# One transfer order, shared score banks and split masks in a fused attention and two-MLP kernel

## The chip, the cores and the metric

The kernel runs on one core of a Trainium2 chip. The metric is the device time of one execution in microseconds; the figure for a kernel is the median of its runs. Below, TensorE, VectorE, ScalarE and GpSimd are the compute engines (PE, DVE, ACT and POOL in the profile), and SP is the engine whose queue issues all transfers between main memory (HBM) and the on-chip memory. TensorE writes its results to eight banks of accumulator memory (PSUM), from which VectorE and ScalarE read them.

## What is computed

```python
# q, k, v: 4 batches, 8 heads, 768 positions, 64 values; weights of the MLPs come as 64-bit floats
k_sum = k.reshape(B, H, nb, 32, D).max(axis=3)        # one key per block of 32
v_sum = v.reshape(B, H, nb, 32, D).mean(axis=3)       # one value per block of 32
scores_l = where(|i - j| < 16, q @ k.T / sqrt(D), -1e9)
scores_s = q @ k_sum.T / sqrt(D) + log(32)
a = softmax(concatenate([scores_l, scores_s]))
x = a @ concatenate([v, v_sum])                       # to 3072 tokens x 512
h = max(max(x @ w1, x @ w2), x @ w3)                  # 768 wide
x2 = h @ w_out
h2 = x2 @ w_in2                                       # 2048 wide
out = (h2 * tanh(softplus(h2))) @ w_out2              # 3072 x 512, fp32
```

A position sees only its neighbours within 15 positions and the 24 block summaries of its batch.

## The kernel before

**Attention.** The 3072 tokens form 24 steps `u` of 128 tokens, six to a batch; a step is two tiles of 64 queries. A tile's keys are a window of 96 positions and 24 block keys, `KX` = 120 columns. `s2(u)` (L427) makes the scores of 8 heads: 32 small fp32 products into the score tile `sc`, then the row maxima `nm` (VectorE) and eight exponentials with their sums (ScalarE). The mask is added in one of two ways. For `u < PEMASK` = 3, TensorE first puts it into `sc` by a product of the identity and the mask (L435), and the scores accumulate on it. From step 3 on, VectorE adds it while it moves the scores to `s` (L452). `s2b` divides by the sums (VectorE for six steps, then GpSimd), `s3` transposes the weights (`ptp`, copied to `pT`), `s4` multiplies by values (`xp`) and splits the result into a rounded part `xh` and a rest `xl`, both fp32r, TensorE's rounded format.

**Numbers in two parts.** Every weight and activation of the MLPs is such a pair, and a product of two is made of three matmuls (high by high, high by low, low by high). `run_job` (L195) brings a weight tile through stages: `fetch` (transfer into `words`, three buffers), `size_of` (ScalarE), `narrow` (VectorE), and a last stage. The first 14 jobs (`PEJOBS`) rebuild the low part by three TensorE products in a bank `wp` (L232 to L234). The second MLP's weights are split in the same way and stored to `w2d` (L256, L257).

**Keys, queries, values.** `load_nat` brings 128 positions into one of four `nat` buffers; `q_prep` and `k_prep` transpose them (`tp`). For batches after the first, `k_prep` copies the transposed keys to `kst`, a single buffer, and stores them to `kTd` (L360); `load_k` later brings a tile's window from there (L396). `v_prep` makes block means of the second batch's values by TensorE (`vp`), copies them to `vc`, which uses the same buffer as `kst`, and stores them to `vsd` (L310). For batches 2 and 3, `make_vsum` makes the means on GpSimd and VectorE. `load_v` brings value windows into four buffers `vr`.

**The MLPs.** The first runs in eight blocks of 384 tokens: `gemm1` with three products `hp` for each of six slices, and `gemm2` with four products `yp`, stored to `x2d` (L623). The second MLP follows: `g3` (product `up`), `mish_a` to `mish_c` (ScalarE and VectorE), `g4` (products `acc`, kept in three banks), and the store of `out`.

**Banks.** During attention: three in `gps` (tag "g": `wp`, `hp`, `yp`), three in `aps` (tag "a": `tp`, `vp`, `ptp`, `xp`) and one tile of two banks in `asc` for the scores. In the second MLP: `gps`, two in `ups`, and three for `acc`.

**Order.** Attention is written as a list of items, five to a step; `attend` emits them between the products of the MLP, about one block and four items ahead. `run_job` is called after every second item at first, before each product for the first two blocks, and before every third product after that. This is program order. A scheduler then places each engine's instructions by its own estimate of when they are ready, and each engine, SP's queue too, runs its own list strictly in that order. Transfers can so leave program order, but for two rules: `behind()` places query, key and value loads and the far key stores behind the last weight transfer while the weights of the first MLP come in, and an engine's instructions that need a buffer wait for its last readers.

Of the kernel before, what the change touches and what calls it, by code (L numbers as in the profile page):

```python
# [19 lines left out]
P = 128  # L20
# [33 lines left out]
def tile_kernel(ctx, tc, q, k, v, w1, w2, w3, w_out, w_in2, w_out2, out):  # L54
# [28 lines left out]
    gps = ctx.enter_context(tc.tile_pool(name="gps", bufs=3, space=PSUM))  # L83
# [43 lines left out]

    att = ExitStack()
# [27 lines left out]
    def fetch(src):  # L156
        words = stage.tile([P, 1024], U32, name="words", tag="words")
        o, x = src(words)
        last["words"] = nc.sync.dma_start(out=o, in_=x)
# [91 lines left out]
    def keep(f, i):  # L251
        def done(w, _):
# [3 lines left out]
            nc.sync.dma_start(out=w2d[f][:, 2 * i], in_=h.bitcast(F32))  # L256
            nc.sync.dma_start(out=w2d[f][:, 2 * i + 1], in_=w)  # L257
# [9 lines left out]
    def load_b(f, tl):  # L267
        wb[f] = tl
        nc.sync.dma_start(out=tl.bitcast(F32), in_=w2d[f])
# [21 lines left out]
    def load_nat(kind, src, b, g):  # L291
        t = ap3.tile([P, H, D], F32, name="nat", tag="nat", bufs=NATB)
        nat[kind, b, g] = t
        with behind() if "words" in last else nullcontext():
            nc.sync.dma_start(out=t, in_=src[b, :, g * P : (g + 1) * P, :].rearrange("h p d -> p h d"))
# [7 lines left out]
    def v_prep(b, g):  # L303
# [4 lines left out]
        vc = ap1.tile([P, H, D], F32, name="vc", tag="kst")[0:NS]  # L308
        nc.scalar.copy(vc, vp[0:NS])
        nc.sync.dma_start(out=vsd[b][:, g * NS : (g + 1) * NS, :].rearrange("h n d -> n h d"), in_=vc)  # L310
# [3 lines left out]
    def load_vsum(b, g, part):  # L314
# [3 lines left out]
        nc.sync.dma_start(out=t[0 : GRP * NB], in_=src[:, part])  # L318

    def make_vsum(b, g, part):  # L320
# [10 lines left out]
        if part == NPART - 1:  # L331
# [5 lines left out]
            nc.sync.dma_start(out=vsd[b][g * GRP : (g + 1) * GRP].rearrange("h n d -> (h n) d"), in_=vs[:, 0])  # L337
# [11 lines left out]
    def k_prep(b, g, st=None):  # L349
# [9 lines left out]
        if b:  # L359
            nc.sync.dma_start(out=kTd[b][:, :, g * P : (g + 1) * P], in_=st)  # L360

    def store_far():

        for g in range(NG):
            lo = max(g * P, NEAR * QT - HALO)
            if lo < (g + 1) * P:
                with behind():
                    nc.sync.dma_start(out=kTd[0][:, :, lo : (g + 1) * P], in_=kst[g][:, :, lo - g * P :])
# [17 lines left out]
    def load_k(T):  # L386
# [9 lines left out]
        nc.sync.dma_start(out=dst[:, :, o : o + hi - lo], in_=kTd[b][:, :, lo:hi])  # L396
# [3 lines left out]
    def load_v(T):  # L400
        b, t = divmod(T, TPS)
        dst = vr[T % RV]
        if T < NEAR:
            if T == 0:
                nc.sync.dma_start(out=dst[NB : NB + HALO], in_=vroom[0][0:HALO])
            for g, l, h, o in pieces(t):
                nc.sync.dma_start(out=dst[o : o + h - l], in_=vroom[g][l:h])
# [3 lines left out]
        nc.sync.dma_start(out=dst[o : o + hi - lo], in_=rows(lo, hi))  # L411

        if o > NB:
            nc.sync.dma_start(out=dst[NB:o], in_=rows(0, o - NB))
# [4 lines left out]
    def load_s(b):  # L419

        for t in vr:
            nc.sync.dma_start(out=t[0:NB], in_=vsd[b].rearrange("h n d -> n h d"))
# [4 lines left out]
    def s2(u):  # L427

        t = u % NG
        mask = masks["first" if t == 0 else "last" if t == NG - 1 else "mid"]  # L430
        sc = asc.tile([P, 2, 512], F32, name="sc", tag="sc")
        add = u >= PEMASK
        if not add:
            for r in range(2):
                nc.tensor.matmul(  # L435
                    sc[:, r, 0 : NP * KX], lhsT=ident, rhs=mask.unsqueeze(1).to_broadcast([P, NP, KX]),
                    start=True, stop=False,
                )
        for p in range(NP):
            for e in reversed(range(GT)):  # L440
                for r in range(2):
# [3 lines left out]
                        sc[c, r, p * KX : (p + 1) * KX], lhsT=qT[u % RQ][d, p, c], rhs=kT[(GT * u + e) % RK][d, p],  # L445
# [3 lines left out]
        src = sc[:, :, 0 : NP * KX].rearrange("q r (p x) -> q r p x", p=NP)  # L449
        if add:  # L450
            wide = mask.unsqueeze(1).unsqueeze(1).to_broadcast([P, 2, NP, KX])
            nc.vector.tensor_tensor(out=heads(s), in0=src, in1=wide, op=ALU.add)  # L452
# [432 lines left out]
```

## Time and profile before

| | |
|---|---|
| median of 3 runs | 1132.33 us (1130.82 to 1132.83) |
| profiled execution | 1133.17 us, span 1131.4 us, mean granted clock 0.994 |
| TensorE matmul | busy 1098.0 us, 97%, 7004 instructions |
| TensorE weight load | 987.8 us, 87% |
| VectorE | 812.4 us, 72%, 1595 instructions |
| ScalarE | 549.6 us, 49%, 1336 instructions |
| GpSimd | 75.8 us, 7%, 132 instructions |
| transfers | 125.49 MB, mean 111 GB/s |

The span reaches from the first instruction to the last; the execution's own time is a little longer. A busy share is a mean over stages that differ: the attention and the first MLP take the time to about 600 us, the second MLP the rest. In the rows shown below, PE is a matmul, PEld the load of its weights, SPq the issue of a transfer by SP; a time in brackets is how long the engine stood idle before the instruction, and behind the arrow is what ended that. A row of stages gives, for each engine, busy time in us and (in brackets) instructions, then the granted TensorE clock, the transfers' share of 16 DMA engines and GB/s. In rows of the chain, the numbers are start and duration. A row of waits has the total in us, the number and the longest.

### The profile page before, as it was taken

The numbers are of one execution on the slowest core, as the hardware profiler recorded it, in microseconds if no ns is written. First come the engines' busy times: TensorE is split into PE (matmuls) and PEld (weight loads), VectorE is DVE, ScalarE is ACT, GpSimd is POOL, SyncE is SP. The second block draws the span as 40 slices with busy tenths as digits, with TensorE's granted clock in tenths as the row PEclk, the third lists the DMA queues.
The fourth block names the chain that finished last, engine by engine and source line by source line (L and its number), as shares of the span: only waits on it lengthen the run. The fifth ranks groups of instructions, "written<-read, shape, count | busy, mean of one in ns | idle before, by whom it ended". The sixth has DMA issues, their size and how long they took to land.

```text
span 1131.4 us, 18637 instructions
## 1 busy us (share of the span) xinstructions
PE 1098.0 (97%) x7004; PEld 987.8 (87%) x7004; DVE 812.4 (72%) x1595; ACT 549.6 (49%) x1336; POOL 75.8 (7%) x132
## 2 busy tenths in 40 slices
PE   6888999999999899999999999999999999999998
PEld 3557889999898899999999998989889898999887
DVE  5678934287887789852238887787878888787775
ACT  4676535345544554632125554545545455454543
POOL 3000012211113110100000000000000000000000
PEclk9999999999999899999999999999999999999999
DMA  9897745466887857521557010100001010000000
GB/s 234 217 253 201 174 126 135 125 172 197 225 215 221 228 172 201 159 68 52 179 189 288 15 57 1 55 2 23 35 1 56 1 29 29 14 29 1 29 1 28
DMA packets 179730, 125.49 MB, mean 111 GB/s; under 512 B 125048, under 2 KB 161400, under 8 KB 177592
## 3 DMA queue, kind: packets, MB, share of 16 engines
q1 hardware_dynamic: 179640, 124.30, 39.0%
q8 instruction: 55, 0.90, 0.3%
q14 instruction: 35, 0.29, 0.1%
HBM read 88.05 MB, written 35.05 MB: 109 GB/s over the span
## 4 chain that ended last, share of the span: by engine, by line
PE 77%; DVE 10%; ACT 5%; DMA 4%; issue 3%; POOL 1%; SPq 0%; ACTq 0%; POOLq 0%; DVEq 0%
PE up L679 8%; PE up L677 8%; PE acc L732 8%; PE up L678 8%; PE acc L733 8%; PE acc L734 8%; PE hp L584 6%; PE hp L586 6%; PE hp L585 6%; ACT s L459 3%; PE yp L618 2%; PE yp L620 2%; PE yp L619 2%; PE xp L493 1%; DVE words L182 1%
## 5 line engine op out<-in xcount | busy, mean ns | idle before, releaser
L695 ACT ACTIVATE r<-n,two 128x384 f32<-128x384 f32 x128 | 78.9, 616 | 153.9 <-DVE n L692 153.9
L584 PE MATMUL hp<-xh,a 128*128 128x384 f32 x384 | 133.9, 349 | 6.3 <-ACT m L592 3.4
L586 PE MATMUL hp<-xh,a 128*128 128x384 f32 x384 | 129.3, 337 | 0.0
L585 PE MATMUL hp<-xl,a 128*128 128x384 f32 x384 | 129.3, 337 | 0.0
L718 DVE TENSOR_TENSOR gl<-g,gh 128x384 fp32r<-128x384 f32 x128 | 71.3, 557 | 64.2 <-ACT gh L717 63.8
L688 ACT ACTIVATE e<-up 128x384 f32<-128x384 f32 x128 | 63.0, 492 | 98.8 <-PE up L679 97.9
L584 PEld LDWEIGHTS hp<-xh,a 128*128 128x128 f32 x384 | 72.4, 188 | 11.1 <-ACT m L592 4.3
L459 ACT ACTIVATE s<-s,nm 128x120 f32<-128x120 f32 x168 | 64.0, 383 | 29.5 <-DVE nm L455 29.5
L705 DVE TENSOR_TENSOR p<-up,r 128x384 f32<-128x384 f32 x128 | 70.6, 552 | 5.5 <-ACT r L696 5.5
L585 PEld LDWEIGHTS hp<-xl,a 128*128 128x128 f32 x384 | 72.5, 189 | 0.8 <-issue 0.5
L586 PEld LDWEIGHTS hp<-xh,a 128*128 128x128 f32 x384 | 72.4, 189 | 0.1
L690 DVE TENSOR_SCALAR ep<-e 128x384 f32<-128x384 f32 x128 | 45.9, 358 | 35.8 <-ACT e L688 35.3
L710 DVE SCALAR_TENSOR_TENSOR g<-u,n 128x384 f32<-128x384 f32 x128 | 70.9, 554 | 0.8
L708 DVE SCALAR_TENSOR_TENSOR u<-u,p 128x384 f32<-128x384 f32 x128 | 70.7, 552 | 0.4
L692 DVE SCALAR_TENSOR_TENSOR n<-e,ep 128x384 f32<-128x384 f32 x128 | 70.7, 552 | 0.3
L707 DVE SCALAR_TENSOR_TENSOR u<-n,r 128x384 f32<-128x384 f32 x128 | 70.3, 549 | 0.0
L717 ACT CAST gh<-g 128x384 fp32r<-128x384 f32 x128 | 64.3, 502 | 9.4 <-DVE g L710 9.4
L584 PE MATMUL hp<-xh,b 128*128 128x384 f32 x192 | 67.8, 353 | 0.3 <-ACT y L622 0.3
L696 ACT ACTIVATE r<-r 128x384 f32<-128x384 f32 x128 | 67.1, 524 | 1.0
L618 PE MATMUL yp<-hh,c 128*128 128x384 f32 x192 | 65.6, 344 | 0.1
L677 PE MATMUL up<-x2h,a 128*128 128x384 f32 x192 | 64.5, 336 | 0.0
L678 PE MATMUL up<-x2l,a 128*128 128x384 f32 x192 | 64.5, 336 | 0.0
(167 smaller groups left out, 2886.0 us busy)
## 6 DMA issues: line engine op xcount, KB each, us to landing
words<-in_moe_w_out SPq DMA_DIRECT2D x22, 512.0 KB, 4.7
words<-in_moe_w SPq DMA_DIRECT2D x18, 512.0 KB, 5.3
words<-in_moe_w_in SPq DMA_DIRECT2D x16, 512.0 KB, 3.9
w2d<-wr SPq DMA_DIRECT2D x32, 256.0 KB, 4.6
w2d<-wa SPq DMA_DIRECT2D x32, 256.0 KB, 5.2
kT<-kTd SPq DMA_DIRECT2D x35, 192.0 KB, 5.1
vr<-in_v SPq DMA_DIRECT2D x35, 192.0 KB, 3.6
nat<-in_q SPq DMA_DIRECT2D x24, 256.0 KB, 4.3
```

Source lines behind the costliest of these rows:

```text
L459: nc.scalar.activation(out=s[:, h], in_=src[:, r, p], func=AF.Exp, bias=nm[:, r, p : p + 1], accum_out=sm[:, h : h + 1])
L584: nc.tensor.matmul(pt[:, :n], lhsT=wh, rhs=xh[:, c, :n], start=(c == 0), stop=False)
L585: nc.tensor.matmul(pt[:, :n], lhsT=wh, rhs=xl[:, c, :n], start=False, stop=False)
L586: nc.tensor.matmul(pt[:, :n], lhsT=wl, rhs=xh[:, c, :n], start=False, stop=(c == KC - 1))
L618: nc.tensor.matmul(pt[:, :n], lhsT=wh, rhs=hh[:, :n], start=(f == 0), stop=False)
L677: nc.tensor.matmul(pt[:, :N2], lhsT=wh, rhs=xh[:, c], start=(c == 0), stop=False)
L678: nc.tensor.matmul(pt[:, :N2], lhsT=wh, rhs=xl[:, c], start=False, stop=False)
L679: nc.tensor.matmul(pt[:, :N2], lhsT=wl, rhs=xh[:, c], start=False, stop=(c == KC - 1))
L695: nc.scalar.activation(out=r, in_=d["n"], func=AF.Ln, bias=two[:, 0:1])
L732: nc.tensor.matmul(o, lhsT=gh[:, c], rhs=w[:, 2], start=(f == 0), stop=False)
L733: nc.tensor.matmul(o, lhsT=gh[:, c], rhs=w[:, 3], start=False, stop=False)
L734: nc.tensor.matmul(o, lhsT=gl[:, c], rhs=w[:, 2], start=False, stop=(f == NF2 - 1))
```

## The change

- **Transfers.** Every transfer goes through a new function `dma`, which places it on SP behind the one before it in program order. `behind()` and `last["early"]` go. At the start, the products of the first scores and one weight job now stand ahead of the first two value loads.
- **Scores.** `sc` becomes two one-bank tiles from the pool `aps`, one for each half of the heads. `asc` goes, `aps` has four banks and `gps` four. VectorE's add, and for steps 0 to 2 its maximum, are done for each half.
- **Masks.** For steps 0 to 2 the mask is split once by VectorE into a rounded part and a rest, in buffers of later `hh5` and `hl5`, and TensorE adds both by fp32r products with the rounded identity `one_r`.
- **Value means.** `v_prep` writes `vc` into the first four partitions of the `nat` buffer that it has read.
- **Second MLP.** `ups` goes; all `up` tiles come from `gps`, four banks where there were five.

```diff
-    gps = ctx.enter_context(tc.tile_pool(name="gps", bufs=3, space=PSUM))
+    gps = ctx.enter_context(tc.tile_pool(name="gps", bufs=4, space=PSUM))
...
+    split_masks = {}
+    for kind, tag in (("first", "hh5"), ("mid", "hl5")):
+        both = gx.tile([P, MAXT * QT], F32R, name=f"both_{kind}", tag=tag)
+        h, l = both[:, 0:KX], both[:, KX : 2 * KX]
+        nc.vector.tensor_copy(h, masks[kind])
+        nc.vector.tensor_tensor(out=l, in0=masks[kind], in1=h.bitcast(F32), op=ALU.subtract)
+        split_masks[kind] = h, l
...
-    aps = att.enter_context(tc.tile_pool(name="aps", bufs=3, space=PSUM))
-    asc = att.enter_context(tc.tile_pool(name="asc", bufs=1, space=PSUM))
-    last = {"early": True}
+    aps = att.enter_context(tc.tile_pool(name="aps", bufs=4, space=PSUM))
+    last = {}
+
+    def dma(out, in_):
+        with tc.issue_after(last["dma"].ins) if "dma" in last else nullcontext():
+            last["dma"] = nc.sync.dma_start(out=out, in_=in_)
...
-        last["words"] = nc.sync.dma_start(out=o, in_=x)
+        dma(out=o, in_=x)
-    def behind():
-        return tc.issue_after(last["words"].ins) if last["early"] else nullcontext()
...
-        vc = ap1.tile([P, H, D], F32, name="vc", tag="kst")[0:NS]
+        vc = t[0:NS]
         nc.scalar.copy(vc, vp[0:NS])
...
-        sc = asc.tile([P, 2, 512], F32, name="sc", tag="sc")
+        sc = [bank("sc") for r in range(2)]
         add = u >= PEMASK
         if not add:
             for r in range(2):
-                nc.tensor.matmul(
-                    sc[:, r, 0 : NP * KX], lhsT=ident, rhs=mask.unsqueeze(1).to_broadcast([P, NP, KX]),
-                    start=True, stop=False,
-                )
+                for j, m in enumerate(split_masks[kind]):
+                    nc.tensor.matmul(
+                        sc[r][:, :, 0:KX], lhsT=one_r, rhs=m.unsqueeze(1).to_broadcast([P, NP, KX]),
+                        start=(j == 0), stop=False,
+                    )
...
         if add:
-            wide = mask.unsqueeze(1).unsqueeze(1).to_broadcast([P, 2, NP, KX])
-            nc.vector.tensor_tensor(out=heads(s), in0=src, in1=wide, op=ALU.add)
-            src = heads(s)
+            for r in range(2):
+                wide = mask.unsqueeze(1).to_broadcast([P, NP, KX])
+                nc.vector.tensor_tensor(out=heads(s)[:, r], in0=src[r], in1=wide, op=ALU.add)
+            src = [heads(s)[:, r] for r in range(2)]
...
-        nc.vector.tensor_reduce(out=nm, in_=src, axis=AX.X, op=ALU.max, negate=True)
+        if add:
+            nc.vector.tensor_reduce(out=nm, in_=heads(s), axis=AX.X, op=ALU.max, negate=True)
+        else:
+            for r in range(2):
+                nc.vector.tensor_reduce(out=nm[:, r], in_=src[r], axis=AX.X, op=ALU.max, negate=True)
...
-        sec["up"] = sec["stack"].enter_context(tc.tile_pool(name="ups", bufs=2, space=PSUM))
...
-        more = (i * NF2 + f) % 5 > 2
-        pt = (sec["up"] if more else gps).tile([P, 512], F32, name="up", tag="g")
+        pt = gps.tile([P, 512], F32, name="up", tag="g")
...
+    run_job()
+    s2(0)
     load_v(0)
     load_v(1)
-    s2(0)
-    run_job()
     s2b(0)
...
-    last["early"] = False
```

In all other places `nc.sync.dma_start(...)` becomes `dma(...)`.

More of the change, by code (lines that the diff above doesn't have):

```diff
@@ L268, in load_b @@
         wb[f] = tl
-        nc.sync.dma_start(out=tl.bitcast(F32), in_=w2d[f])
+        dma(out=tl.bitcast(F32), in_=w2d[f])
     kTd = [dpool.tile([P, NP, S], F32, name=f"kTd{b}") for b in range(B)]
@@ L293, in load_nat @@
         nat[kind, b, g] = t
-        with behind() if "words" in last else nullcontext():
-            nc.sync.dma_start(out=t, in_=src[b, :, g * P : (g + 1) * P, :].rearrange("h p d -> p h d"))
+        dma(out=t, in_=src[b, :, g * P : (g + 1) * P, :].rearrange("h p d -> p h d"))
     def mean_v(out, t, first, n, start, stop):
@@ L317, in load_vsum @@
         src = v[b, g * GRP : (g + 1) * GRP].rearrange("h (n u j) d -> (h n) u j d", j=HB, u=NPART)
-        nc.sync.dma_start(out=t[0 : GRP * NB], in_=src[:, part])
+        dma(out=t[0 : GRP * NB], in_=src[:, part])
     def make_vsum(b, g, part):
@@ L359, in k_prep @@
         if b:
-            nc.sync.dma_start(out=kTd[b][:, :, g * P : (g + 1) * P], in_=st)
+            dma(out=kTd[b][:, :, g * P : (g + 1) * P], in_=st)
     def store_far():
@@ L366, in store_far @@
             if lo < (g + 1) * P:
-                with behind():
-                    nc.sync.dma_start(out=kTd[0][:, :, lo : (g + 1) * P], in_=kst[g][:, :, lo - g * P :])
+                dma(out=kTd[0][:, :, lo : (g + 1) * P], in_=kst[g][:, :, lo - g * P :])
     def q_prep(b, g):
@@ L395, in load_k @@
         lo, hi, o = window(t, WIN)
-        nc.sync.dma_start(out=dst[:, :, o : o + hi - lo], in_=kTd[b][:, :, lo:hi])
+        dma(out=dst[:, :, o : o + hi - lo], in_=kTd[b][:, :, lo:hi])
         if b and t < RK:
@@ L410, in load_v @@
         lo, hi, o = window(t, WIN)
-        nc.sync.dma_start(out=dst[o : o + hi - lo], in_=rows(lo, hi))
+        dma(out=dst[o : o + hi - lo], in_=rows(lo, hi))
         if o > NB:
-            nc.sync.dma_start(out=dst[NB:o], in_=rows(0, o - NB))
+            dma(out=dst[NB:o], in_=rows(0, o - NB))
     def bank(name):
@@ L421, in load_s @@
         for t in vr:
-            nc.sync.dma_start(out=t[0:NB], in_=vsd[b].rearrange("h n d -> n h d"))
+            dma(out=t[0:NB], in_=vsd[b].rearrange("h n d -> n h d"))
     att_t = {}
@@ L429, in s2 @@
         t = u % NG
-        mask = masks["first" if t == 0 else "last" if t == NG - 1 else "mid"]
-        sc = asc.tile([P, 2, 512], F32, name="sc", tag="sc")
+        kind = "first" if t == 0 else "last" if t == NG - 1 else "mid"
+        mask = masks[kind]
+        sc = [bank("sc") for r in range(2)]
         add = u >= PEMASK
@@ L459, in s2 @@
             nc.scalar.activation(
-                out=s[:, h], in_=src[:, r, p], func=AF.Exp, bias=nm[:, r, p : p + 1], accum_out=sm[:, h : h + 1]
+                out=s[:, h], in_=src[r][:, p], func=AF.Exp, bias=nm[:, r, p : p + 1], accum_out=sm[:, h : h + 1]
             )
@@ L622, in emit @@
             last["act"] = nc.scalar.copy(y[:, :n], pt[:, :n])
-            nc.sync.dma_start(out=x2d[i][:, e, :], in_=y[:, :n])
+            dma(out=x2d[i][:, e, :], in_=y[:, :n])
         return [emit]
@@ L653, in load_x2 @@
             n = min(N2 - done, sizes[j] * QT - o)
-            nc.sync.dma_start(out=x[:, done : done + n], in_=x2d[j][:, c, o : o + n])
+            dma(out=x[:, done : done + n], in_=x2d[j][:, c, o : o + n])
             done += n
@@ L738, in g4 @@
                 r0 = i * N2 + m * P
-                nc.sync.dma_start(out=out[r0 : r0 + P, :], in_=ob)
+                dma(out=out[r0 : r0 + P, :], in_=ob)
     room = [wpool.tile([P, 4, 512], F32, name=f"room{i}", tag=f"c{i}") for i in range(3)]
@@ L749, in tile_kernel @@
         nat["k", 0, g] = t = room[g].rearrange("p (h d) -> p h d", h=H)
-        nc.sync.dma_start(out=t, in_=k[0, :, g * P : (g + 1) * P, :].rearrange("h p d -> p h d"))
+        dma(out=t, in_=k[0, :, g * P : (g + 1) * P, :].rearrange("h p d -> p h d"))
         if g == 2:
@@ L754, in tile_kernel @@
     for g in range(NG):
-        nc.sync.dma_start(out=vroom[g], in_=v[0, :, g * P : (g + 1) * P, :].rearrange("h p d -> p h d"))
+        dma(out=vroom[g], in_=v[0, :, g * P : (g + 1) * P, :].rearrange("h p d -> p h d"))
         if g == 2:
```

16 lines of the change are left out of this document (8 added, 8 removed).

## The prediction

> **What bounds the kernel now.** I read the page's slices first, then the busy times by stage, then the chain that ended last in the first 60 us, then the waits.
>
> ```profile
> span 1131.4 us, 18637 instructions
> DMA  9897745466887857521557010100001010000000
> ```
> ```profile
> core 0: us, PE busy (x) PEld busy (x) DVE busy (x) ACT busy (x) POOL busy (x), PEclk, DMA share, GB/s
> 0.00:20.00 20.00, 12.09 (x68) 7.17 (x68) 8.05 (x13) 7.62 (x14) 10.91 (x51) 1.00 0.93 223
> 20.00:40.00 20.00, 18.18 (x81) 8.15 (x82) 14.25 (x27) 13.27 (x47) 1.72 (x3) 0.91 0.72 192
> 40.00:80.00 40.00, 32.19 (x324) 20.63 (x323) 31.87 (x59) 29.43 (x86) 0.00 (x0) 0.96 1.13 259
> 80.00:100.00 20.00, 16.35 (x111) 13.16 (x109) 14.88 (x28) 12.43 (x34) 0.00 (x0) 1.00 0.76 204
> 100.00:140.00 40.00, 39.98 (x318) 33.91 (x319) 39.23 (x76) 23.91 (x56) 2.92 (x5) 1.00 0.75 190
> 140.00:300.00 160.00, 158.20 (x1279) 148.72 (x1278) 91.57 (x159) 67.98 (x205) 27.38 (x38) 1.00 0.59 156
> 300.00:400.00 100.00, 94.32 (x743) 87.49 (x742) 79.55 (x138) 50.17 (x149) 23.62 (x30) 0.97 0.80 218
> 400.00:560.00 160.00, 160.00 (x1229) 154.25 (x1228) 96.53 (x167) 65.09 (x177) 9.21 (x5) 1.00 0.46 141
> 560.00:1131.40 571.40, 566.75 (x2863) 514.35 (x2861) 436.43 (x934) 279.66 (x575) 0.00 (x0) 1.00 0.13 45
> ```
>
> TensorE is full from 400 us to the end but for 4.65 us, the tail behind the last product. It is idle 21.2 us in the first 100 us (20+20+40+20 less 12.09, 18.18, 32.19 and 16.35) and 1.80 + 5.68 = 7.5 us between 140 and 400. So whatever the change does off TensorE, the time moves only by what it does to these 28.7 us, and by what it removes from TensorE while that is the limit. The digits of the DMA line show why the front has holes: transfers are dense early, with weights, keys, queries and values all wanted at once, and the 40 to 80 us row gives a share of 1.13. The 100 to 140 us row has VectorE (39.23 of 40) and TensorE both full.
>
> The chain in the first 60 us:
>
> ```profile
> 7.29 3.57 PE sc L435 x4
> 19.97 2.86 ACT s L459 x16
> 22.88 3.43 PE sc L435 x4
> 27.21 5.26 PE vp L298 x12
> 34.48 0.90 PE wp L232 x2
> 37.25 5.26 DMA words<-in_moe_w
> ```
> ```profile
> 26.65 0.78 SPq L295 DMA_DIRECT2D nat<-in_q  x1
> 35.45 0.37 SPq L159 DMA_DIRECT2D words<-in_moe_w  x1
> ```
>
> The reader is to see that the mask products (L435) stand on it twice, for 3.57 and 3.43 us, and that the second begins when the exponentials of step 0 end (19.97 + 2.86 = 22.83), because the score tile is a single buffer. Behind it wait the value means, the products of a weight job (wp), and so the weight slot and the next weight transfer: SP issues nothing between 27.4 and 35.45.
>
> **The change part by part.**
>
> *Masks as two rounded parts.* Only steps 0 to 2 use TensorE for masks. Each has two fp32 products, which show as four records; after, four fp32r products of 480 columns. Prices:
>
> ```profile
> 39.15 1.88 PE L435 MATMUL sc<-mask_mid,ident 128*128 128x480 f32 x4
> 96.66 0.39 PE L233 MATMUL wp<-wr,one_r 128*128 128x512 f32 x1
> 96.89 0.39 PE L234 MATMUL wp<-a,neg_r 128*128 128x512 f32 x1
> ```
>
> Two fp32r products of 512 columns begin 0.23 us apart, so 480 columns take 0.22 and four 0.86 us. The same four records took 3.57 us at 7.29 and 1.88 at 39.15, 1.9 times apart, so at the slow pace I reckon 1.64. Step 0 then saves 3.57 - 1.64 = 1.9, less about 0.6 for the two new VectorE instructions between the mask and its product (120 elements each; they lie between nothing and the 0.68 us that the 512-element row below takes): 1.3. Step 2 saves 1.88 - 0.86 = 1.0, off the chain above; I take half, 0.5.
>
> *Scores in two of four shared banks.* The mask product of step 1 no longer waits for the exponentials of step 0; it can run in TensorE's idle time before 22.88. Between 1.8 (3.43 - 1.64, still in line) and 3.43 leaves the chain: I take 2.8, nearer the upper end because TensorE waited just there for VectorE:
>
> ```profile
> 21.51 1.17 PE L232 MATMUL wp<-words,ident 128*128 128x512 f32 x2 [1.86 <-DVE words L182]
> ```
>
> The front gains 1.3 + 2.8 + 0.5 = 4.6 us. Bounds: nothing, if transfers or VectorE set the front anyway, and 1.9 + 3.43 + 1.0 = 6.3.
>
> Here a rule may speak against it. The records at 7.29 and 39.15 differ 1.9 times with the same work, while PEclk reads 1.00 in the first row of stages. The Trainium skill, page "TensorE: Matmul & The Clock Gate", section "What's actually happening", says that the array runs at half clock until it has been busy for some 3.4 us, and falls back after such an idle time; the two rows agree. By that page the shorter masks also take away activity ahead of the value means, which might then begin cold: an estimate of 1.7 us back (3.4 us at half pace), and a sum 1.7 us higher. I don't take it: the means at 27.21 follow other products, as they will after.
>
> The price of sharing: tp, vp, ptp and xp had three banks and the scores two of their own; now all share four. Nearest row, a transpose that waited for a bank:
>
> ```profile
> 100.02 0.66 PE L344 MATMUL tp<-ident,nat 128*128 128x128 f32 x4 [1.17 <-ACT vc L309]
> ```
>
> Bounds 0 and 3 us (one or two such waits in the crowded 50 to 100 us, one at most later); I take 0.6.
>
> *A fourth gps bank.* The first MLP's products rotate through gps: three banks before, four after. The waits for a bank in the hole between 300 and 400:
>
> ```profile
> 353.67 0.44 PE L584 MATMUL hp<-xh,b 128*128 128x384 f32 x1 [0.29 <-ACT y L622]
> 358.44 0.44 PE L584 MATMUL hp<-xh,a 128*128 128x384 f32 x1 [2.15 <-ACT m L592]
> 370.31 0.44 PE L584 MATMUL hp<-xh,a 128*128 128x384 f32 x1 [0.40 <-DVE m L596]
> 379.84 0.44 PE L584 MATMUL hp<-xh,a 128*128 128x384 f32 x1 [1.87 <-DVE m L596]
> 97.30 0.33 PE L584 MATMUL hp<-xh,b 128*128 128x384 f32 x1
> 97.47 0.33 PE L585 MATMUL hp<-xl,b 128*128 128x384 f32 x1
> ```
>
> They sum to 4.71 us. A product is 12 matmuls 0.17 apart, about 2.1 us, which is how much further TensorE may run with one more bank: it covers nearly each of them. I take 4.0. Bounds: 0, if the late evacuation returns as a wait for xh or hl, and 7.5, all idle time between 140 and 400. In the second MLP five up banks become four. A tile begun at 791.09 is last read at 801.34 + 0.55, and the tile four further on begins at 807.82:
>
> ```profile
> 791.09 0.33 PE L677 MATMUL up<-x2h,a 128*128 128x384 f32 x1
> 801.34 0.55 DVE L705 TENSOR_TENSOR p<-up,r 128x384 f32<-128x384 f32 x1
> 807.82 0.34 PE L677 MATMUL up<-x2h,b 128*128 128x384 f32 x1
> ```
>
> 5.9 us to spare; I cost it at nothing, covered by the products between.
>
> *Value means in place.* vc leaves the kst buffer, whose key store it waited for; the wait of 1.17 us at 100.02 goes: 1.2 gained, between 0 and 1.2. The nat slot is now held until the small store has landed, and a later nat load on SP waits for it; with four slots and loads a step ahead I take nothing.
>
> *Two adds for one on VectorE, from step 3 on, 21 times.*
>
> ```profile
> 371.62 0.68 DVE L503 TENSOR_TENSOR xl<-xp,xh 128x512 fp32r<-128x512 f32 x1
> 374.99 1.15 DVE L452 TENSOR_TENSOR s<-sc,mask_last 128x960 f32<-128x960 f32 x1
> ```
>
> 448 more elements cost 0.47 us, so 480 take 0.65 and two halves 1.29: 0.14 more, 3.0 us over 21 steps. The three steps between 100 and 140 us, where VectorE is full, put 0.4 on the path; TensorE hides the rest. The split maxima of steps 0 to 2 add the same 0.14 each and lie in idle time of VectorE.
>
> *Transfers in program order.* Nothing is added to the 443 transfers; their order on SP changes, and any that waits holds all later ones. Program order puts the two key stores of a step side by side, and the second waits for the first to land, since kst is one buffer. Then come queries, keys and weight transfers, and behind these VectorE's narrowing and the wp and hp products.
>
> ```profile
> 61.89 0.77 SPq L360 DMA_DIRECT2D kTd<-kst  x1
> 64.32 1.58 SPq L159 DMA_DIRECT2D words<-in_moe_w  x2
> 171.96 5.09 SPq L360 DMA_DIRECT2D kTd<-kst  x2
> ```
>
> At 61.89 a lone store passes and two weight transfers follow within 4 us. At 171.96 two stand together and hold SP 5.09 us, of which some 4 is waiting. The front has three such pairs (keys of the second batch), so the cost is 12 us if all of it reaches TensorE. At 171.96 nothing did, in a stage 98.9% full. The keys' own loads, far ahead of program order now, come later, and value copies for tiles 4 and 5 wait for the first xp; both are wanted a step later. On the other side, key and x2d stores go out sooner, and ScalarE waits less for them:
>
> ```profile
> ACT y L622 <- DMA x2d<-y: 16.8, 5, 4.1
> ```
>
> Bounds: 3 us gained and 12 lost. I take 3.5 lost, nearer the covered row, since transfers already queued (share 1.13) go on while SP waits.
>
> *Sum.* -4.6 - 4.0 - 1.2 + 0.6 + 0.4 + 3.5 = -5.3 us. The profiled execution took 1133.17 us, so 1127.9 against it; it stood 0.84 above the median of the runs, 1132.33, and on that scale the time is 1127.0.
>
> **The rivals.**
>
> *SP is held by stores (slower).* The place: the key-store pairs of the second batch, between 50 and 110 us. If weights are what TensorE waits for there, the 12 us arrive whole and the 4.6 us of the front are lost as well, since masks out of the way only uncover the same weights: -4.0 - 1.2 + 0.6 + 0.4 + 12 = +7.8, 1140.1 us. It decides from 6.5 us of holding on. For it: the chain passes through a weight transfer of 5.26 us at 37.25. Against: 21 us of idle time give room.
>
> *The front doesn't follow (no change).* Masks leave the chain, but VectorE or the transfers set the front: -4.0 - 1.2 + 0.6 + 0.4 + 3.5 = -0.7, 1131.6. For it: VectorE is at 39.23 of 40 from 100 to 140, with the same work. Against: SP's silence from 27.4 to 35.45 is TensorE's doing.
>
> *Order helps (faster still).* Stores in order free y, kst and the banks behind them: all 7.5 us between 140 and 400 go, the holding costs nothing: -4.6 - 7.5 - 1.2 + 0.6 + 0.4 = -12.3, 1120.0. For it: the 16.8 us that ScalarE waited for x2d stores. Against: waits on landings of weight stores remain.
>
> **How the numbers follow.** Forecast 0.42, its own range 1122 to 1131; stores 0.25; front 0.18; order 0.15. A measurement of this kernel can tell about 0.2%, 2.3 us, from no change. Most of the forecast and all of the last case are faster: 0.55. The front case and an edge of the forecast are no change: 0.19. The stores leave 0.26 for slower. The range runs from 1115, below the order case by its bank bound, to 1141, just over the stores case.
>
> **What would show it.** Right: four L435-like products under 2 us at each of steps 0 to 2, that of step 1 begun before the last exponential of step 0; SP's silence after 27 us ending 3 to 5 us sooner; the hp waits of 300 to 400 gone; 571 us still from 560 to the end at the same fill. Wrong: SP waiting for kst pairs while TensorE waits for words between 50 and 110 us; more bank waits at tp or sc; TensorE under 98% after 400 us.

## The result, and the profile after

| | before | after |
|---|---|---|
| median, same chip | 1131.69 us (1130.82 to 1132.83, 4 runs) | 1161.93 us (1158.91 to 1162.75, 4 runs) |
| ratio | | 1.0262 (95%: 1.0240 to 1.0283) |
| profiled span, mean granted clock | 1131.4 us, 0.994 | 1160.9 us, 0.976 |
| TensorE matmul busy | 1098.0 us | 1102.0 us |

The change makes the kernel 30 us slower; 1127.0 was forecast, with 1141 as the upper end. First the rows by stage of the changed kernel (busy time and number for each engine, then clock, the transfers' share and GB/s):

```profile
0.00:20.00 20.00, 10.94 (x68) 7.66 (x68) 9.50 (x18) 10.12 (x29) 10.38 (x51) 0.98 0.93 225
20.00:40.00 20.00, 16.36 (x80) 7.82 (x80) 13.62 (x25) 10.05 (x27) 2.18 (x3) 0.85 0.79 186
40.00:80.00 40.00, 27.32 (x230) 18.68 (x230) 23.44 (x44) 23.22 (x67) 0.00 (x0) 0.80 0.72 174
80.00:100.00 20.00, 16.49 (x101) 12.70 (x101) 13.37 (x26) 11.64 (x33) 0.00 (x0) 0.89 0.64 155
100.00:140.00 40.00, 39.46 (x326) 36.02 (x324) 34.78 (x69) 19.72 (x49) 1.74 (x4) 1.00 0.71 187
140.00:300.00 160.00, 154.90 (x1263) 144.87 (x1255) 95.52 (x174) 75.50 (x229) 30.51 (x37) 0.99 0.63 158
300.00:400.00 100.00, 89.27 (x676) 85.28 (x675) 67.76 (x125) 40.89 (x109) 17.74 (x21) 0.93 0.70 183
400.00:560.00 160.00, 151.02 (x1244) 144.06 (x1244) 114.55 (x201) 71.71 (x210) 18.33 (x17) 0.97 0.55 154
560.00:1160.90 600.90, 596.30 (x3033) 543.93 (x3032) 441.81 (x946) 286.57 (x588) 0.00 (x0) 1.00 0.15 52
```

TensorE stands idle 28.9 us in the first 100 us (21.2 before), 15.8 us from 140 to 400 (7.5 before) and 9.0 us from 400 to 560, where before it had none. With 0.5 us from 100 to 140 and an unchanged tail, that is 25.5 of the 29.5 us. The other 4 us are longer busy time, and the clock reads lower: 0.80 from 40 to 80 us, 0.96 before. From 40 to 80 us transfers take a share of 0.72 where they took 1.13. So they are not too many; they begin too late. The queue of SP shows where (start and duration of the issue; the gaps between rows aren't printed):

```profile
57.78 0.96 SPq L148 DMA_DIRECT2D words<-in_moe_w  x1
65.32 7.24 SPq L148 DMA_DIRECT2D kTd<-kst  x2
72.66 0.58 SPq L148 DMA_DIRECT2D nat<-in_q  x1
...
84.76 2.39 SPq L148 DMA_DIRECT2D words<-in_moe_w  x2
91.08 0.56 SPq L148 DMA_DIRECT2D kTd<-kst  x1
```

From 58.74 to 72.56 SP does nothing but two key stores, and from 87.15 to 91.08 it waits for the next. What each key store waits for stands in ScalarE's and TensorE's lists:

```profile
58.72 2.07 PE L241 MATMUL wp<-words,ident 128*128 128x512 f32 x2 [4.60 <-DVE words L191]
...
61.57 1.88 PE L453 MATMUL sc<-kT,qT 64*64 64x120 f32 x32
...
63.38 1.24 PE L352 MATMUL tp<-ident,nat 128*128 128x128 f32 x8
...
64.46 1.07 PE L241 MATMUL wp<-words,ident 128*128 128x512 f32 x2
...
64.72 0.58 ACT L363 COPY kst<-tp 128x512 f32<-128x512 f32 x1
...
67.89 0.40 ACT L473 ACTIVATE s<-s,nm 128x120 f32<-128x120 f32 x1 [0.41 <-DVE nm L466]
...
71.39 0.58 ACT L363 COPY kst<-tp 128x512 f32<-128x512 f32 x1
```

The transposes behind the first copy stand on TensorE behind a weight product that waited 4.60 us and behind the scores of step 3. The second copy stands on ScalarE behind that step's eight exponentials. So the key copies wait for weights, and the next weights wait on SP for the key copies. The view of waits has it in sums (total, times, longest); SP's own:

```profile
SPq L148 <- ACT y L636: 102.0, 17, 37.6
...
SPq L148 <- ACT kst L363: 47.7, 9, 8.7
SPq L148 <- ACT wr L263: 39.9, 14, 7.5
```

and the engines', after and then the one row of before:

```profile
ACT wa L178 <- DMA w2d<-wa: 36.7, 15, 4.5
...
PE wp L241 <- DVE words L191: 13.3, 3, 5.9
...
PE sc L453 <- DMA kT<-kTd: 9.3, 4, 4.6
```
```profile
ACT wa L169 <- DMA w2d<-wa: 5.7, 7, 1.6
```

SP's own of before, for the same three (each transfer has a line of its own there, so smaller rows of other lines belong to them too):

```profile
SPq L623 <- ACT y L622: 42.1, 15, 6.5
...
SPq L256 <- ACT wr L254: 11.9, 19, 2.7
...
SPq L360 <- ACT kst L355: 7.4, 3, 3.9
```

SP waits for x2 (y), keys (kst) and split weights (wr), and longer than before for each: with the smaller rows of before, it was 48.7, 8.8 and 13.0 us. The largest row of this view, 468.7 us for the output, belongs to the second MLP, where TensorE is full. ScalarE then waits 36.7 us, not 5.7, until the split weights of a buffer have landed, and TensorE waits for key windows (the last row of after), for which it has no row before. Behind 560 us TensorE is as full as before: 4.60 us idle against 4.65.

### The profile page after: what moved, and what is told of

It is laid out like the page before. It is cut to its first block, busy times and chain, and to the rows that moved or that the text cites. A ratio compares the mean times of both kernels' runs of the same rounds, so it can differ in the third digit from the quotient of the medians.

```text
span 1160.9 us, 18582 instructions
## 1 busy us (share of the span) xinstructions
PE 1102.0 (95%) x7004; PEld 1001.0 (86%) x7004; DVE 814.3 (70%) x1623; ACT 549.4 (47%) x1336; POOL 80.9 (7%) x132
## 4 chain that ended last, share of the span: by engine, by line
PE 69%; DVE 11%; DMA 9%; ACT 5%; issue 3%; SPq 2%; POOL 0%; ACTq 0%; DVEq 0%; POOLq 0%
PE up L691 8%; PE up L689 8%; PE acc L744 8%; PE up L690 8%; PE acc L745 8%; PE acc L746 8%; PE hp L598 5%; PE hp L599 5%; PE hp L600 4%; SPq L148 2%; ACT s L473 2%; DMA w2d<-wa 1%; PE yp L634 1%; DMA words<-in_moe_w 1%; DVE words L191 1%
## 5 line engine op out<-in xcount | busy, mean ns | idle before, releaser
L599 PE MATMUL hp<-xl,a 128*128 128x384 f32 x384 | 132.2, 344 | 0.0
L598 PEld LDWEIGHTS hp<-xh,a 128*128 128x128 f32 x384 | 73.9, 192 | 5.3 <-ACT m L606 3.5
L600 PEld LDWEIGHTS hp<-xh,a 128*128 128x128 f32 x384 | 74.3, 194 | 1.0 <-issue 0.9
L473 ACT ACTIVATE s<-s,nm 128x120 f32<-128x120 f32 x168 | 64.0, 382 | 23.3 <-DVE nm L466 23.3
L178 ACT ACTIVATE wa<-words 128x512 f32<-128x512 f32 x56 | 37.7, 674 | 62.1 <-DMA w2d<-wa 36.7
L633 PE MATMUL yp<-hl,c 128*128 128x384 f32 x192 | 65.7, 343 | 0.8 <-DVE hl L618 0.8
```

The lines of the kernel that those rows point to most:

```text
L473: nc.scalar.activation(out=s[:, h], in_=src[r][:, p], func=AF.Exp, bias=nm[:, r, p : p + 1], accum_out=sm[:, h : h + 1])
L598: nc.tensor.matmul(pt[:, :n], lhsT=wh, rhs=xh[:, c, :n], start=(c == 0), stop=False)
L599: nc.tensor.matmul(pt[:, :n], lhsT=wh, rhs=xl[:, c, :n], start=False, stop=False)
L600: nc.tensor.matmul(pt[:, :n], lhsT=wl, rhs=xh[:, c, :n], start=False, stop=(c == KC - 1))
```

## The experiments

All ratios are to the kernel before on the same chip, whose medians there were 1130.4 to 1131.7 us; in brackets the 95% interval. "Chain" is the rule that every transfer is issued behind the one ahead of it in program order. The two arrangements of banks are called shared (after) and separate (before).

**Order alone, and the change without it.** First, the kernel before with the chain, and with the two value loads moved behind the first scores as in the changed kernel:

```diff
-        last["words"] = nc.sync.dma_start(out=o, in_=x)
+        dma(out=o, in_=x)
...
```

> The kernel before with the change of transfers alone (one chain in program order, and the first scores and one weight job ahead of the first two value loads); banks, masks and value means as before. Theory O (the order costs the time): 1150 to 1170 us, 2 to 3% slower than before, SP waiting in front of the pairs of key stores for 6 us and more each. Theory B (shared banks and what hangs on them cost it): 1125 to 1140 us.

Measured: 1142.77 us, 1.0110 (1.0093 to 1.0127), between the ranges of the two theories: the order alone makes a part of the loss. Second, the changed kernel with the transfers as before:

```diff
-        with tc.issue_after(last["dma"].ins) if "dma" in last else nullcontext():
-            last["dma"] = nc.sync.dma_start(out=out, in_=in_)
+        return nc.sync.dma_start(out=out, in_=in_)
+
+    def behind():
...
```

> The changed kernel with the order of the kernel before put back (no chain, loads placed behind the last weight transfer at first, value loads ahead of the first scores); banks, masks and value means as changed. Theory O: 1120 to 1132 us, as fast as before or faster. Theory B: 1150 to 1165 us.

Measured: 1126.39 us, 0.9960 (0.9946 to 0.9974). The chain turns a gain of about 5 us into a loss of 30. It costs 11.6 us in the kernel before (16.0 with the split masks and the value means in place, below) and 35.5 in the changed one, so order and banks work on each other. The profiled spans of the changed kernel without and with the chain (1127.5 and 1160.9 us) differ by 33.4 us: 21.1 are idle time of TensorE, 12.3 longer busy time for the same products (1089.7 and 1102.0 us).

**Which transfers.** In the changed kernel, the key stores of batches 1 to 3 are taken out of the chain:

```diff
-            dma(out=kTd[b][:, :, g * P : (g + 1) * P], in_=st)
+            nc.sync.dma_start(out=kTd[b][:, :, g * P : (g + 1) * P], in_=st)
```

> The changed kernel with the key stores of batches 1 to 3 left out of the chain: the scheduler places them, all other transfers stay in program order. Theory O, pairs: 1135 to 1148 us. Theory O, all: 1150 to 1160 us. Theory B: 1160 us.

Measured: 1138.63 us, 1.0084 (1.0058 to 1.0110). Next, the same for all stores (keys, value means, split weights, x2, output), so that the chain holds the loads alone:

```diff
-            dma(out=w2d[f][:, 2 * i], in_=h.bitcast(F32))
+            nc.sync.dma_start(out=w2d[f][:, 2 * i], in_=h.bitcast(F32))
...
-            dma(out=x2d[i][:, e, :], in_=y[:, :n])
+            nc.sync.dma_start(out=x2d[i][:, e, :], in_=y[:, :n])
...
```

> The changed kernel with only the loads in the chain: all stores (keys, means, w2d, x2d, out) are placed by the scheduler. Theory S (stores that wait for their producers hold the loads behind them): 1124 to 1132 us, like the kernel without a chain (1126.4). If loads in program order are themselves late (keys and values taken only at their place): 1134 to 1140 us, like the kernel with key stores free (1138.6).

Measured: 1128.54 us, 0.9985 (0.9973 to 0.9998). Against no chain the loads in program order cost 2 to 3 us, with intervals that just overlap. The rest of the loss is stores, taken out in this order: 23 us those of keys, 10 us the others. Was it the landing of the first key store, for which the second copy into the single buffer waits, as the prediction's step had it? The next kernel writes the transposed keys back into the buffer that they came from, and no copy waits for a store:

```diff
-            st = ap1.tile([P, NP, P], F32, name="kst", tag="kst")
+            st = t.rearrange("p (a r) d -> p a (r d)", a=NP)
```

> The changed kernel, with the transposed keys written back into their own nat buffer instead of the single kst buffer, so that the second key store of a step no longer waits for the first to land; the chain stays. If the pairs of key stores make the loss (theory O, pairs): 1138 to 1150 us, and no SP issue row of two key stores longer than 2 us. If any transfer that waits does it (theory O, all): 1153 to 1162 us. Theory B: 1160 us.

Measured: 1158.50 us, 1.0249 (1.0227 to 1.0270): 3.4 us of 35. Its row on SP hardly moves:

```profile
64.85 6.83 SPq L148 DMA_DIRECT2D kTd<-nat  x2
```

The landing was not what held SP; the place of the copy in ScalarE's list was.

**Why the banks matter.** The changed kernel, chain and all, with the banks and the score tile of before:

```diff
-    aps = att.enter_context(tc.tile_pool(name="aps", bufs=4, space=PSUM))
+    aps = att.enter_context(tc.tile_pool(name="aps", bufs=3, space=PSUM))
+    asc = att.enter_context(tc.tile_pool(name="asc", bufs=1, space=PSUM))
```

> The changed kernel with banks and scores as before (three gps, three aps, one score tile of two banks, one add of 960 elements, five up banks); program order, rounded masks and means in place stay. Theory K (in program order the shared banks make key transposes and so key stores later, and SP waits for these): 1138 to 1146 us, like the order alone (1142.8). If masks or means in place make the rest of the loss: 1155 to 1163 us.

Measured: 1139.49 us, 1.0078 (1.0053 to 1.0103). Its rows at the same place:

```profile
49.24 1.51 PE L353 MATMUL tp<-ident,nat 128*128 128x128 f32 x9
...
50.41 0.59 ACT L364 COPY kst<-tp 128x512 f32<-128x512 f32 x1
...
55.51 7.65 SPq L149 DMA_DIRECT2D kTd<-kst  x2
...
57.66 1.05 PE L454 MATMUL sc<-kT,qT 64*64 64x120 f32 x32 [0.53 <-DMA kT<-kTd]
```

Here the key transposes stand ahead of the scores of step 3, the first copy is done 14 us sooner and its store needs no wait. The second still holds SP to 63.16. Two kernels tell whether this is a matter of how many banks there are or of who shares them. Both have three gps banks and the two extra up banks of before. The first has five shared banks:

```diff
-    gps = ctx.enter_context(tc.tile_pool(name="gps", bufs=4, space=PSUM))
+    gps = ctx.enter_context(tc.tile_pool(name="gps", bufs=3, space=PSUM))
-    aps = att.enter_context(tc.tile_pool(name="aps", bufs=4, space=PSUM))
+    aps = att.enter_context(tc.tile_pool(name="aps", bufs=5, space=PSUM))
```

> As the changed kernel, but five banks shared by scores, tp, vp, ptp and xp, three in gps, and two extra up banks in the second MLP as before: the same eight banks as in the kernel with separate score banks, which took 1139.5 us. Theory 'ring' (order of handing out, not the number of banks): the key transposes still stand behind the scores of step 3; the time stays at 1155 to 1165. Rival 'bank count': a fifth bank relieves the waits for a bank, and the time falls by more than 10 us, towards 1140.

Measured: 1159.18 us, 1.0252 (1.0233 to 1.0272). The second leaves the scores in four shared banks, but gives the transposes one of their own:

```diff
-        tp = aps.tile([P, NP, P], F32, name="tp", tag="a")
+        tp = apt.tile([P, NP, P], F32, name="tp", tag="tp")
```

> As the changed kernel, all transfers in one chain, but the transposes of keys and queries (tp) have a bank of their own; scores, ptp, vp and xp share four; to make room, three gps banks, and the second MLP's up tiles take two more as before. Theory 'ring': the shared banks hurt under the chain because banks of one pool are handed out in the order of the program, so the key transposes of the second batch had to stand behind the scores of step 3 and the weight job ahead of them; with a bank of their own they begin before those scores, at about 50 us and not at 63.4, the first key store no longer holds SP from 57.8 to 65.3, and the time falls from 1161.9 to near that of the chain with separate score banks, 1139.5 (1135 to 1146). Rival 'bank count': four banks are too few for five kinds of tile; one fewer gps bank then makes it no better, 1158 to 1165.

Measured: 1143.90 us, 1.0107 (1.0093 to 1.0122). One row of SP in the five-bank kernel, and then three rows of the other:

```profile
64.29 5.49 SPq L148 DMA_DIRECT2D kTd<-kst  x2
```
```profile
53.90 0.58 ACT L364 COPY kst<-tp 128x512 f32<-128x512 f32 x1 [0.79 <-PE tp L353]
...
55.67 7.13 SPq L149 DMA_DIRECT2D kTd<-kst  x2
...
58.38 1.05 PE L454 MATMUL sc<-kT,qT 64*64 64x120 f32 x32
```

A fifth bank changes nothing that can be seen; a bank that isn't shared with the scores brings 18 of the 22 us. In a common pool the key transposes come behind the scores that precede them in the program, in a pool of their own they pass them. This is the pool's doing and not the chain's: in the changed kernel without the chain the key copies begin as late (64.49 and 72.59 us, against 64.72 and 71.39), but there a weight transfer goes out at 63.05, ahead of the first key store at 66.47, and the time is 1126.4 us.

**The rest of the chain's price, with separate banks.** The kernel with the banks of before (1139.5), and only the loads in the chain, by the edit shown above for all stores:

> The changed kernel with separate score banks as before (1139.5 us), and only the loads in the chain; all stores (keys, value means, split weights, x2, output) go where the scheduler puts them. Theory: the chain costs what the stores in it hold, with separate banks too; the time falls to near the kernel with the same banks and no chain, 1123.5 (1121 to 1128). Rival: the order of the loads themselves costs a part of the 16 us (keys, queries and values behind weights); then 1130 to 1138.

Measured: 1119.00 us, 0.9896 (0.9870 to 0.9923), the fastest kernel here and a little under the range. Against the same banks with no chain (0.9931, 0.9917 to 0.9944) the intervals just overlap. Into it the key stores are put back:

```diff
-            nc.sync.dma_start(out=kTd[b][:, :, g * P : (g + 1) * P], in_=st)
+            dma(out=kTd[b][:, :, g * P : (g + 1) * P], in_=st)
```

> The kernel with separate score banks and only the loads in the chain (1119.0 us), with the key stores of batches 1 to 3 put back into the chain. Theory: 12 us more, 1131 (1128 to 1134). Rival: key stores are all of the 20.5 us: 1137 to 1140; other rival: few of it: 1120 to 1125.

Measured: 1130.60 us, 0.9995 (0.9976 to 1.0014). And the whole chain without the key stores, by the reverse of this edit in the kernel that took 1139.5 us:

> The changed kernel with separate score banks as before (1139.5 us), the key stores of batches 1 to 3 out of the chain, all other transfers in it. Theory: the prediction's bound of 12 us is right for the key stores and the rest, some 8 us, is the stores of the split weights and of x2, between 140 and 560 us: 1127.5 (1125 to 1131). Rival: key stores are all of it: 1119 to 1122; other rival: the later stores are most of it: 1133 to 1138.

Measured: 1131.61 us, 1.0000 (0.9984 to 1.0016), a little over the range of the theory: the later stores cost more than it said. In one table (us, masks and value means as changed in all):

| in the chain | nothing | loads | loads, key stores | all but key stores | all |
|---|---|---|---|---|---|
| separate banks | 1123.5 | 1119.0 | 1130.6 | 1131.6 | 1139.5 |
| shared banks | 1126.4 | 1128.5 | not run | 1138.6 | 1161.9 |

Each added to the loads alone, with separate banks key stores cost 11.6 us and the other stores 12.6; both together cost 20.5. Key stores taken out of the whole chain bring 7.9 us there. The stages show where. In the kernels with loads, loads and key stores, and all but key stores, one after the other:

```profile
0.00:100.00 100.00, 81.88 (x616) 55.31 (x617) 72.64 (x136) 64.69 (x172) 14.41 (x56) 0.95 0.91 228
...
300.00:400.00 100.00, 98.31 (x831) 92.46 (x830) 85.86 (x149) 50.13 (x148) 24.26 (x30) 1.00 0.82 227
```
```profile
0.00:100.00 100.00, 79.72 (x570) 53.82 (x571) 68.69 (x128) 61.55 (x166) 13.95 (x54) 0.93 0.87 214
...
300.00:400.00 100.00, 91.98 (x727) 85.35 (x725) 81.16 (x141) 50.10 (x148) 23.92 (x30) 0.97 0.79 218
```
```profile
0.00:100.00 100.00, 81.75 (x620) 55.40 (x621) 74.12 (x136) 64.76 (x173) 16.04 (x58) 0.98 0.94 229
...
300.00:400.00 100.00, 91.25 (x752) 85.45 (x752) 79.85 (x142) 49.95 (x148) 24.14 (x30) 0.98 0.76 211
```

Key stores leave TensorE 2.2 us more idle time in the first 100 us and 6.3 from 300 to 400; the other stores nothing in the front and 7.1 from 300 to 400. Over the whole span it is 6.4 us more idle time and 5.4 us longer busy time for key stores, 9.1 and 2.6 for the others (TensorE busy 1086.3, 1091.7 and 1088.9 us). For the other stores, one row that grows is ScalarE's wait for the landing of split weights, first in the kernel with loads alone, then in the one with all but key stores:

```profile
ACT wa L179 <- DMA w2d<-wa: 4.7, 3, 1.7
```
```profile
ACT wa L179 <- DMA w2d<-wa: 35.0, 18, 4.2
```

A store of split weights that waits its turn on SP frees its buffer late, and the next weights come late. Only 8.9 of the 35.0 us lie between 300 and 400 us (1.5 with loads alone), and TensorE's own waits there are mostly for VectorE and ScalarE to empty its banks. So the way from this wait to TensorE's idle time is argued, not shown, and which weighs more, split weights or x2, stays open.

**The other parts of the change.** In the changed kernel with the chain, the masks of before (one fp32 product for each half), and then vc in the key buffer as before:

```diff
-                for j, m in enumerate(split_masks[kind]):
...
+                nc.tensor.matmul(
+                    sc[r][:, :, 0:KX], lhsT=ident, rhs=mask.unsqueeze(1).to_broadcast([P, NP, KX]),
...
```

> The changed kernel with the masks of steps 0 to 2 added by one fp32 product each, as before, into the shared banks; the rest as changed. Theory K: 1156 to 1166 us. Rival M (the masks' two parts upset the front, where TensorE stood 5.9 us for a weight job at 17 us): 1138 to 1148 us.

```diff
-        vc = t[0:NS]
+        vc = ap1.tile([P, H, D], F32, name="vc", tag="kst")[0:NS]
```

> The changed kernel with the value means in the kst buffer again; the rest as changed. Theory K: 1158 to 1166 us. Rival V (means in place hold nat buffers until their store lands, and the chain waits for that; SP waited 13.0 us for vsd stores): 1138 to 1150 us.

Measured: 1157.99 us, 1.0246 (1.0224 to 1.0268), and 1162.31 us, 1.0279 (1.0259 to 1.0299). Neither explains the loss: the intervals of both overlap with that of the changed kernel, and by the medians the masks of before take off 4 us, the other edit nothing. Their worth is seen without the chain. No chain and the banks of before, the two edits of the sections above together:

> The changed kernel without the chain (1126.4 us) and with the banks of the kernel before: three gps banks, scores in a tile of two own banks, five up banks; only the split masks and the value means in place are left of the change. Theory of the prediction's terms: the fourth gps bank and the second score tile are worth 4.0 + 2.8 - 1.0 of the gain; then the gain of 4.7 against before falls to about 1.5, 1129.5 (1127 to 1132). Rival: the gain is that of the masks and of vc; the time stays at 1126.4 (1125 to 1128).

Measured: 1123.48 us, 0.9931 (0.9917 to 0.9944), below both ranges: the banks of before are the better ones. The shared banks, no chain, and the masks of before, by the edit just shown:

> The changed kernel without the chain (1126.4 us), with the masks of before (one fp32 product of identity and mask for each half) in the shared banks. Theory of the prediction: the shorter products are worth about 1.3 + 0.6 + 0.5 us in the front; 1128.8 (1127.5 to 1130). Rival: the front is set by weights and VectorE, shorter masks are worth nothing, and the two split instructions on VectorE are saved; 1126 (1124.5 to 1127.5).

Measured: 1126.24 us, 0.9953 (0.9941 to 0.9966). And each of the two edits alone, in the kernel before:

```diff
-        vc = ap1.tile([P, H, D], F32, name="vc", tag="kst")[0:NS]
+        vc = t[0:NS]
```

> The kernel before with one edit: the value means vc are written into the buffer that they were read from, not into the single key buffer. The prediction's term: 1.2 us gained, about 1130 against 1131.1. Rival: freeing the key buffer moves key copies and stores forward, and most of the 7.6 us of the unchained kernel with separate banks is here: 1124 to 1127.

```diff
-                nc.tensor.matmul(
-                    sc[:, r, 0 : NP * KX], lhsT=ident, rhs=mask.unsqueeze(1).to_broadcast([P, NP, KX]),
...
+                for j, m in enumerate(split_masks["first" if t == 0 else "mid"]):
+                    nc.tensor.matmul(
+                        sc[:, r, 0 : NP * KX], lhsT=one_r, rhs=m.unsqueeze(1).to_broadcast([P, NP, KX]),
...
```

> The kernel before with one edit: the masks of steps 0 to 2 as two rounded parts, in the score tile of before. The prediction's terms without the second score tile: 1.3 + 1.8 + 0.5 = 3.6 us gained, 1127.5 (1126.5 to 1129). Rival: no more than 1 us, since with the shared banks the old masks cost nothing (1126.2 against 1126.4): 1130 to 1132.

Measured: value means in place 1125.60 us, 0.9950 (0.9932 to 0.9969); masks 1129.83 us, 0.9983 (0.9968 to 0.9998). By these ratios that is 5.7 and 1.9 us, and their sum 7.6 is the gain of the unchained kernel with separate banks (0.9931, 7.8 us). Last, that kernel with the keys written back in place, by the edit of `st` shown above:

> The changed kernel without the chain and with the banks of before (1123.5 us), and the transposed keys written back into the buffer that they were read from, so that a key copy never waits for the store ahead of it to land. Theory: without the chain the scheduler keeps the two stores apart and this wait is hidden; no change, 1122 to 1125. Rival: the waits are still paid in part, 1119 to 1122.

Measured: 1127.91 us, 0.9970 (0.9955 to 0.9986), no gain but a loss of 4 us, outside both ranges. A buffer that its next load needs is then held until a store has landed: in this kernel SP waits 14.4 us, 12 times, for key stores to land (kTd from nat), and in the kernel with the copy in kst not once. How much of the 4 us comes from this isn't shown.

## Why the prediction was wrong, step by step

- **Transfers in program order: the step that failed.** It took 3.5 us, between 3 gained and 12 lost; the chain costs 35.5 us in this kernel. That is 32 of the 35 us between forecast and result; without the chain the other terms sum to -8.8 us, and the kernel gained 4.5 (0.9960). Three things were wrong in it. (1) The value was taken from the row at 171.96, where a pair of stores held SP and cost nothing, with the reason that queued transfers go on meanwhile. In the front they run dry: the share from 40 to 80 us falls from 1.13 to 0.72. With separate banks the key stores added to the loads cost 11.6 us. That this is near the upper bound of 12 is partly luck: the bound stood for three pairs in the front, and of the 11.6 us the front shows 2.2 as idle time and the stage from 300 to 400 us 6.3. (2) Only key stores were priced, as a wait for a landing. The other stores were costed at nothing; they cost 12.6 us (10.1 with shared banks); with separate banks 7.1 of it is idle time from 300 to 400 us, where the prediction saw only waits for banks. (3) The terms were added as if they didn't touch. With shared banks the first key copy comes 14 us later, and taking the key stores out of the whole chain brings 23.3 us, not 7.9.
- **Sharing: +0.6, bounds 0 and 3.** Without the chain the exchange of banks (fourth gps bank, scores, maxima in halves) costs 2.9 us, 1126.4 against 1123.5, clear of the noise by a hair (the intervals of the two ratios end at 0.9944 and begin at 0.9946), where the terms for it (-4.0, a second score tile, +0.6, +0.4) summed to a gain. The fourth gps bank does what was said. First the groups of TensorE from 300 to 400 us with three gps banks and separate scores, then with four and shared ones, both without the chain:

```profile
L598 PE MATMUL hp<-xh,a 128*128 128x384 f32 x72 | 25.7, 357 | 4.6 <-DVE m L610 3.4 <-ACT m L606 1.2
```
```profile
L602 PE MATMUL hp<-xh,a 128*128 128x384 f32 x79 | 27.5, 348 | 0.1
...
L497 PE MATMUL ptp<-ident,s 128*120 128x128 f32 x40 | 5.9, 274 | 2.8 <-DVE s L466 2.3 <-DVE xl L521 0.6
...
L355 PE MATMUL tp<-ident,nat 128*128 128x128 f32 x36 | 5.2, 277 | 0.6 <-DVE s L466 0.4 <-DVE xl L521 0.2
```

  The wait of 4.6 us for an evacuated bank falls to 0.1, and 3.4 us come back as transposes that wait for a shared bank, most of it (2.7) for VectorE to empty the scores. So this stage still gains 1.4 us (TensorE busy 96.19 us against 94.81); the loss lies elsewhere, with 2.7 us more idle time in the first 100 us, 3.2 more from 140 to 300 and 1.8 more from 400 to 560. The prediction had asked for this only as "more bank waits at tp or sc".
- **Masks: -4.6.** Worth 1.9 us alone (0.2 to 3.6 by the interval), where the terms without the second score tile give 3.6; with shared banks no worth can be seen (0.9960, and 0.9953 with the masks of before). In the changed kernel the products of steps 0 and 1 became shorter, but those of step 2, at 44.20 behind a hole of 3.28 us, did not (1.88 before), and those of step 1 did not move ahead of the value means, which begin at 25.92:

```profile
11.72 1.48 PE L444 MATMUL sc<-both_first,one_r 128*128 128x480 f32 x4
...
23.06 2.07 PE L241 MATMUL wp<-words,ident 128*128 128x512 f32 x2 [5.88 <-DVE words L191]
...
31.29 1.15 PE L444 MATMUL sc<-both_mid,one_r 128*128 128x480 f32 x4
...
44.20 1.97 PE L444 MATMUL sc<-both_mid,one_r 128*128 128x480 f32 x4
...
19.88 0.17 DVE L481 TENSOR_SCALAR esum<-esum 128x8 f32<-128x8 f32 x1 [2.35 <-ACT s L473]
...
35.88 1.73 SPq L148 DMA_DIRECT2D words<-in_moe_w  x2
```

  TensorE waits 5.88 us for a weight job's words, to 23.06. VectorE's list shows why: it stands idle 2.35 us until the exponentials of step 0 end at 19.88, divides that step, and only at 21.40 begins on those words; before, it began on them at 19.85, ahead of the division. So the exponentials still hold the front, now through VectorE, the mask of step 1 comes at 31.29, and SP's silence ends at 35.88 (35.45 before). With the masks alone, in the score tile of before, the value means do begin sooner, at 23.38 and not 27.14, but the silence ends only 1.25 us sooner, at 34.20. The second rival, "the front doesn't follow", was right about the masks.
- **Value means in place: -1.2, named as the upper bound.** Alone it brings 5.7 us. The term was read off TensorE's wait of 1.17 us; a row nearer to the price is ScalarE's, which the prediction did not look at:

```profile
ACT vc L309 <- DMA kTd<-kst: 5.3, 2, 2.9
```

  In that time ScalarE holds up all its list. The row is gone with the edit, and TensorE's idle time from 80 to 100 us, where the first of the two waits lies (to 99.40), falls from 3.65 to 0.56 us; where the rest of the 5.7 us comes from isn't shown. Under the chain the gain is lost (1162.3 against 1161.9).
- **VectorE's two adds** take 0.65 us each, as worked out (1.29 against 1.15):

```profile
L462 DVE TENSOR_TENSOR s<-sc,mask_mid 128x480 f32<-128x480 f32 x28 | 17.2, 651 | 9.3 <-PE sc L453 9.3
```

- **Four up banks** cost nothing: idle time behind 560 us is unchanged.
- **The slow-clock sentence.** The Trainium skill, page "TensorE: Matmul & The Clock Gate", section "What's actually happening", lets the array run at half clock after some 3.4 us of idling. The pair of products behind the wait of 4.60 us takes 2.07 us and the same pair without a wait 1.07 (at 64.46), which agrees. The prediction set this aside for the masks, rightly: the value means took 5.44 us, 5.33 before. Holes made by SP may be paid twice through it. The longer busy time fits this, 4 us against the kernel before and 12.3 against the changed kernel without the chain, but no run separates it: with the order alone the mean clock fell too (0.986 from 0.994), and the busy time did not grow (1098.1 against 1098.0 us).
- **The rivals.** "SP is held by stores" had the right sign and mechanism; its price of 12 us is near what key stores cost with separate banks and half of what they cost with shared ones, and its place, the front, was a part only. It had a chance of 0.25. What it lacked were the later stages, the other stores, and that the copies themselves would come later. The Trainium skill, page "DMA: Bandwidth & Descriptors", section "Anatomy of one DMA — SWDGE (gpsimd) path", says that a wait on a semaphore takes place on the issuing sequencer before dispatch. The sentence stands under the GpSimd path; SP's gap from 58.74 to 65.32 agrees with it for SP's queue.

## What to carry to other kernels

On a queue that issues in order, a store is as late as the engine that makes its data, and every load behind it is as late as the store: let stores pass. Here loads in order with free stores gave 1119.0 us, everything in order 1139.5, with the same banks. Whether the loads should be ordered stays open: against no chain it was 4 us better with separate banks and 2 us worse with shared ones, both near the noise. Before putting two kinds of tile into one pool, ask which of them waits for the other by program order, and whether something on a queue waits for the later one; costs that meet at the same engine cannot be added one by one.

## What the runs showed that was not expected

- A shared pool can cost by order and not by number: five shared banks took 1159.2 us, four and one apart 1143.9.
- A tiny copy (4 x 512 elements, 0.57 us) that waited 5.3 us in two places on ScalarE went to another buffer, and this was worth 5.7 us of the whole, three times as much as the masks by the medians.
